# A transformer block on one core: the second part of k laid out over both partition halves without pinned matmuls, and every block of probabilities multiplied in two rounded parts

## The chip, the cores and the metric

The kernel runs on 1 core of one Trainium2 chip. The metric is the device time of one execution in microseconds (us). Three runs of the kernel before took 474.45, 476.0 and 477.67 us; the median is 476.0 us.

## The reference

Three blocks follow each other. First comes local attention with block summaries (2 batches, 8 heads, 768 positions, head size 64). Its output feeds the block that this change is about, a causal attention with four experts of 64 dimensions each, over two batches of 768 positions:

```python
for e in range(E):                       # E = 4 experts, K = 2 chosen per position
    q = x @ wq[e]; k = x @ wk[e]; v = x @ wv[e]
    scores = scale * (q @ k.transpose(0, 2, 1))
    scores = np.where(causal, -1e9, scores)
    scores = scores - scores.max(-1, keepdims=True)
    a = np.exp(scores); a /= a.sum(-1, keepdims=True) + 1e-09
    ye = a @ v @ wo[e]
    out += weight_of_expert_e_at_each_position * ye
```

A token and channel mixer follows: `u = x + relu(xt @ w_tok1) @ w_tok2` and `out = u + relu(u @ w_ch1) @ w_ch2`. The four mixer weights arrive as 64-bit floats, whose bits the kernel decodes on the chip.

## The kernel before, in words

**Precision.** Most operands are kept as two rounded parts, hi and lo, that TensorE takes at the rate of a single pass (the type fp32r in the trace). A product then is two or three such matmuls that add up in one PSUM bank. `split` (L91 to L93) makes the parts: ScalarE copies hi out of PSUM, VectorE writes lo as the difference. A matmul on plain float32 operands is one instruction in the program and two records in the trace.

**Stages.** `s1` is the local attention of one batch. `proj` makes q, k and v of the experts, `attn` the expert attention, `tokmix` the token mixer, `chmix` the channel mixer in passes of three weight blocks, and `load_ch` and `wt_load` load and decode weights. Decoding (`decode_w`, L115 to L135) is a ring of two raw buffers: a DMA from SyncE, then ScalarE, GpSimd, VectorE, ScalarE, GpSimd; the next load of a buffer waits for the last reader.

**What sets the order.** `run` interleaves generators when the program is written down: attention of batch 0 with the projection of batch 1 and the decoding of token weights, then attention of batch 1 with the token mixer, the decoding of the first channel weights and the first channel pass. A scheduler then orders every engine's instructions by its own model of their durations and picks buffers of the pools by when it thinks they come free. On the chip each engine goes through its list in that order. All DMAs are issued by SyncE, one after the other.

**Scores.** For experts e = 0 to 3 and the two halves h of the positions, `attn` computes scores of three row tiles. Two experts share the tiles of one pair p. `q2[p]` holds, for one expert, the hi part of q in the expert's own 64 partitions and the lo part in the other 64; `k2[p]` holds the hi part of k in both halves. So one matmul over 128 partitions (L368) gives (q hi + q lo) times k hi. The lo part of k is not copied: a second matmul (L366) reads the 64 partitions of `k2l` in which the projection left it, against q hi alone. Pins (`keep_in_program_order`) hold the matmuls of a group of two banks in a fixed order: first the 128-partition ones, then the 64-partition ones, then the pieces that share a bank. For h = 0 these are pieces of 128, 256 and 384 columns; for h = 1 pieces of 512, 128 and 256 columns in a first group and two of 512 in a second. VectorE masks each piece and takes its minimum (L374), ScalarE takes the exponential (L378), GpSimd normalises (L384).

**Values.** TensorE transposes each 128-wide block of probabilities (L394). Most blocks are split into `ph` and `pl` and multiplied with V in two matmuls (L404, L405). Blocks j = 0 and 3 of batch 0 and j = 3 of batch 1 instead are copied whole by ScalarE as `pf` (L398) and multiplied once as float32 (L399). That is 16 blocks, all 384 columns wide.

**Pools.** Big tiles have tag "b" (11 buffers of 6 KB per partition), half tiles tag "hf" (6 of 3 KB). The lo parts of k live in half tiles until their pair of experts is done.

Of the kernel before, what the change touches and what calls it, by code (L numbers as in the profile page):

```python
# [25 lines left out]
P = 128  # L26
# [3 lines left out]
NB = 3  # L30
NCH = NC1 // P // NB

NBIG, XB, MB, HB = 11, 8, 6, 6
BK = {"sc": 3, "pt": 3, "acc": 2}
NEGB = -8.0e9
BIG = 3.0e38
# [6 lines left out]
def stack_kernel(ctx: ExitStack, tc, qT, kT, kwT, vw, vT, wqkv, wo, tok1, tok2, ch1, ch2,  # L43
# [30 lines left out]
    def half(shape, dt, name):  # L74
        return big.tile(shape, dt, tag="hf", name=name, bufs=HB)
# [62 lines left out]
    def s1_load(b, hp, qb):  # L138
        first = b == 0 and hp == 0
        kx = unit([P, NT, KX], F32, f"kx{b}{hp}")  # L140
        kt = None
        if first:

            kt = xunit([P, S + 2 * WIN], F32, "kt")
            vec.memset(kx[:, 0, KW:KX], 0.0)
        vt = half([P, S], F32, "vt")
        vx = unit([P, NT, P], F32, f"vx{b}{hp}")
        loads = [(kt, kT) if first else (kx, kwT[b, hp])]
        loads += [(qb[i::2, :, i, :], qT[b, hp, i::2].rearrange("p (t c) -> p t c", c=P)) for i in range(2)]
# [124 lines left out]


    def proj(b, xh, xl, out):
        q2 = [unit([P, 2, S], F32R, f"q2{b}{i}") for i in range(2)]
        k2 = [unit([P, 2, S], F32R, f"k2{b}{i}") for i in range(2)]
        V = [unit([P, ST, 2, P], F32R, f"V{b}{i}") for i in range(2)]
        k2l = [None, None]  # L280
        out.extend((q2, k2, k2l, V))
        lg = gp.tile([P, ST, NE], F32, name="lg", bufs=1)
        for st in range(ST):
# [35 lines left out]


        for p in range(2):
            for c0, dst in ((0, q2), (1, k2)):
                hi, lo = (half([P, S], F32R, f"s{b}{p}{c0}{x}") for x in "hl")
                for h in range(2):
# [7 lines left out]
                    if h == 1:  # L332
                        for e in range(2):
                            own, other = slice(64 * e, 64 * e + 64), slice(64 - 64 * e, 128 - 64 * e)
                            nc.sync.dma_start(dst[p][own, e, :].bitcast(F32), hi[own].bitcast(F32))
                            nc.sync.dma_start(dst[p][other, e, :].bitcast(F32), (lo, hi)[c0][own].bitcast(F32))
                    yield
                if c0:
                    k2l[p] = lo

    def attn(b, q2, k2, k2l, V, wg, yT):
        for e in range(NE):
            pp, e0 = e // 2, 64 * (e % 2)
            es = slice(e0, e0 + 64)
            for h in range(2):
# [5 lines left out]
                    nk = P * (3 * h + r + 1)  # L351
                    prs.append((pre if h == 0 else sp).tile([P, nk], F32, name=f"pr{nk}", bufs=2))


                for gi, group in enumerate(((((0, 0, 128, 0), (1, 0, 256, 128)), ((2, 0, 384, 0),)),) if h == 0 else
                                           ((((0, 0, 512, 0),), ((1, 0, 128, 0), (2, 0, 256, 128))),
                                            (((1, 128, 640, 0),), ((2, 256, 768, 0),)))):
                    todo = [(a[:, o:o + c1 - c0], r, c0, c1, o > 0) for i, ts in enumerate(group)
                            for a in (bank("sc", f"s2s{b}{e}{h}{gi}{i}"),) for r, c0, c1, o in ts]

                    steps = [(t, 0) for t in todo if not t[4]] + [(t, 1) for t in todo if not t[4]]
                    steps += [(t, low) for t in todo if t[4] for low in (1, 0)]
                    for i, ((a, r, c0, c1, sec), low) in enumerate(steps):
                        qs = slice(P * (3 * h + r), P * (3 * h + r) + P)
                        if low:
                            mm = ten.matmul(a, q2[pp][es, e % 2, qs], k2l[pp][es, c0:c1], start=sec, stop=not sec)  # L366
                        else:
                            mm = ten.matmul(a, q2[pp][:, e % 2, qs], k2[pp][:, e % 2, c0:c1], start=not sec, stop=sec)  # L368
                        if i:
                            tc.keep_in_program_order(mm)  # L370
                    for a, r, c0, c1, _ in todo:
                        nk = P * (3 * h + r + 1)
                        ci, n = int(c0 > 0), c1 - c0
                        vec.tensor_tensor_reduce(prs[r][:, c0:c1], a, cmask[:, 512 - n:] if c1 == nk else cmask[:, :n],  # L374
                                                 scale=-0.125, scalar=mn[:, r, 0:1] if ci else BIG,
                                                 op0=ALU.add, op1=ALU.min, accum_out=mn[:, r, ci:ci + 1])
                        if c1 == nk:
# [11 lines left out]
                for j in range(nj):  # L389
# [3 lines left out]
                    for r in range(r0, 3):  # L393
                        ten.transpose(pT[:, P * r:P * r + P], prs[r][:, P * j:P * j + P], ident)  # L394
                    v = V[pp][:, j, e % 2, :]
                    if j in ((0, 3), (3,))[b]:
                        pf = sp.tile([P, HALF], F32, tag="ph", name="pf", bufs=3)
                        act.activation(pf[:, c0:], pT[:, c0:HALF], AF.Copy)  # L398
                        ten.matmul(acc[:, c0:HALF], v.bitcast(F32), pf[:, c0:], start=j == 0, stop=j == nj - 1)  # L399
                        continue  # L400
                    ph = sp.tile([P, HALF], F32R, tag="ph", name="ph", bufs=3)
                    pl = sp.tile([P, HALF], F32R, tag="pl", name="pl", bufs=3)
                    split(ph[:, c0:], pl[:, c0:], pT[:, c0:HALF])
# [264 lines left out]
```

## Time and profile before

| what | value |
|---|---|
| median of the runs shown | 476.0 us |
| the profiled execution's own time | 473.83 us |
| its span, first to last instruction | 471.9 us |
| PE busy / DVE / ACT / POOL | 446.6 / 283.5 / 231.0 / 283.3 us |
| mean granted TensorE clock | 0.980 of 2.4 GHz |
| chain that ended last, by engine | PE 79%, DMA 9%, DVE 5%, ACT 2%, issue 2%, POOL 1%, SP queue 1% |

PE is TensorE, DVE VectorE, ACT ScalarE, POOL GpSimd, SP SyncE. A matmul's record starts when it is issued and lasts through its pipeline, so two neighbouring records overlap, and a busy PE is not a PE at its peak. What a matmul costs in a stream is read from start to start. The chain of waits goes back from the last instruction to whatever released each step. In order of time the program has four stages: the inputs and local attention until about 94 us, attention of batch 0 until about 180 us, attention of batch 1 with the token mixer until about 250 us, and channel passes to the end.

### The profile page before, as it was taken

The numbers are of one execution on the slowest core, as the hardware profiler recorded it, in microseconds if no ns is written. First come the engines' busy times: TensorE is split into PE (matmuls) and PEld (weight loads), VectorE is DVE, ScalarE is ACT, GpSimd is POOL, SyncE is SP. The second block draws the span as 40 slices with busy tenths as digits, with TensorE's granted clock in tenths as the row PEclk, the third lists the DMA queues.
The fourth block names the chain that finished last, engine by engine and source line by source line (L and its number), as shares of the span: only waits on it lengthen the run. The fifth ranks groups of instructions, "written<-read, shape, count | busy, mean of one in ns | idle before, by whom it ended". The sixth has DMA issues, their size and how long they took to land.

```text
span 471.9 us, 8309 instructions
## 1 busy us (share of the span) xinstructions
PE 446.6 (95%) x2920; PEld 415.6 (88%) x2920; DVE 283.5 (60%) x821; ACT 231.0 (49%) x653; POOL 283.3 (60%) x319
## 2 busy tenths in 40 slices
PE   3778999999999998999999999999999999999996
PEld 3667999888787676889899999999999999999996
DVE  6777775658668749797796642645672673322322
ACT  1574975777777568868664333233323321110110
POOL 5664652658887875978895889787873772000000
PEclk9797999999999899999999999999999999999999
DMA  9999917504312932211211111212221110001111
GB/s 269 330 278 290 303 33 205 111 2 128 96 46 63 228 90 67 90 45 46 68 46 67 45 46 45 75 60 90 61 75 44 46 44 1 1 0 68 67 68 67
DMA packets 27704, 44.90 MB, mean 95 GB/s; under 512 B 2192, under 2 KB 19344, under 8 KB 27664
## 3 DMA queue, kind: packets, MB, share of 16 engines
q1 hardware_dynamic: 27664, 44.38, 32.4%
q8 instruction: 23, 0.38, 0.3%
q14 instruction: 17, 0.14, 0.1%
HBM read 34.93 MB, written 3.15 MB: 81 GB/s over the span
## 4 chain that ended last, share of the span: by engine, by line
PE 79%; DMA 9%; DVE 5%; ACT 2%; issue 2%; POOL 1%; SPq 1%; DVEq 0%; ACTq 0%
PE o L100 7%; PE h L101 7%; PE h L102 7%; PE o L101 7%; PE o L102 7%; PE h L100 7%; PE s1s L196 3%; DMA vt<-in_vT_dram 3%; PE s2p L394 3%; PE s2s L366 2%; DMA raw<-in_ch_dram 2%; PE s2s L368 2%; PE s1a L235 2%; PE pj L100 2%; PE s2a L399 2%; PE pj L102 2%
## 5 line engine op out<-in xcount | busy, mean ns | idle before, releaser
L96 ACT ACTIVATE hh<-h 128x384 fp32r<-128x384 f32 x48 | 23.5, 490 | 95.7 <-PE h L102 95.3
L126 POOL TENSOR_SCALAR deca<-deca 128x512 f32<-128x512 f32 x30 | 58.6, 1959 | 12.8 <-ACT deca L125 12.2
L101 PE MATMUL o<-hl,c2h 128*128 128x384 f32 x192 | 64.2, 336 | 0.0
L102 PE MATMUL o<-hh,c2l 128*128 128x384 f32 x192 | 64.2, 336 | 0.0
L497 DVE TENSOR_TENSOR oa<-o,oa 128x384 f32<-128x384 f32 x64 | 32.0, 549 | 52.7 <-PE o L102 52.7
L97 DVE SCALAR_TENSOR_TENSOR hl<-h,hh 128x384 fp32r<-128x384 f32 x48 | 26.4, 554 | 44.2 <-ACT hh L96 44.1
L100 PE MATMUL o<-hh,c2h 128*128 128x384 f32 x192 | 49.4, 336 | 0.0
L132 POOL TENSOR_TENSOR raw<-raw 128x512 f32<-128x512 f32 x30 | 32.3, 1076 | 25.8 <-DVE raw L129 23.5
L196 PE MATMUL s1s<-kx,qb 128*128 128x120 f32 x192 | 33.2, 337 | 13.0 <-DVE wvl L112 7.7
L208 ACT ACTIVATE pr<-n,mn 128x120 f32<-128x120 f32 x96 | 36.5, 383 | 15.2 <-DVE mn L205 15.2
L196 PEld LDWEIGHTS s1s<-kx,qb 128*128 128x128 f32 x192 | 31.1, 246 | 13.9 <-DVE wvl L112 7.7
L133 POOL TENSOR_TENSOR deca<-deca,raw 128x512 f32<-128x512 f32 x30 | 39.7, 1324 | 1.1
L384 POOL TENSOR_SCALAR pr<-pr,f,wg 128x128 f32<-128x128 f32 (+5 forms) x48 | 37.5, 791 | 2.0 <-DVE f L381 2.0
L101 PEld LDWEIGHTS o<-hl,c2h 128*128 128x128 f32 x192 | 36.0, 188 | 0.1
L102 PEld LDWEIGHTS o<-hh,c2l 128*128 128x128 f32 x192 | 36.0, 188 | 0.0
L131 ACT ACTIVATE raw<-raw 128x512 f32<-128x512 uint32 x30 | 20.2, 675 | 32.1 <-DMA raw<-in_ch_dram 30.8
L378 ACT ACTIVATE pr<-pr,mn 128x384 f32<-128x384 f32 (+5 forms) x48 | 31.8, 664 | 6.9 <-DVE mn L374 6.8
L100 PEld LDWEIGHTS o<-hh,c2h 128*128 128x128 f32 x192 | 34.8, 188 | 0.1
L100 PE MATMUL h<-u0h,c1h 128*128 128x384 f32 x96 | 32.5, 338 | 0.0
L101 PE MATMUL h<-u0l,c1h 128*128 128x384 f32 x96 | 32.4, 337 | 0.0
L100 PE MATMUL h<-u1h,c1h 128*128 128x384 f32 x96 | 32.3, 336 | 0.0
L102 PE MATMUL h<-u1h,c1l 128*128 128x384 f32 x96 | 32.3, 336 | 0.0
(206 smaller groups left out, 1296.5 us busy)
## 6 DMA issues: line engine op xcount, KB each, us to landing
raw<-in_ch_dram SPq DMA_DIRECT2D x24, 512.0 KB, 3.5
kx<-in_kwT_dram SPq DMA_DIRECT2D x7, 720.0 KB, 10.1
vx<-in_vw_dram SPq DMA_DIRECT2D x8, 576.0 KB, 10.5
qb<-in_qT_dram SPq DMA_DIRECT2D x16, 192.0 KB, 8.7
vt<-in_vT_dram SPq DMA_DIRECT2D x8, 384.0 KB, 10.1
raw<-in_tok_dram SPq DMA_DIRECT2D x6, 512.0 KB, 4.5
out_dram<-oa SPq DMA_DIRECT2D x16, 192.0 KB, 2.0
rqk<-in_wqkv_dram SPq DMA_DIRECT2D x4, 256.0 KB, 10.2
```

Source lines behind the costliest of these rows:

```text
L97: vec.scalar_tensor_tensor(lo, src, 0.0, hi.bitcast(F32), op0=ALU.max, op1=ALU.subtract)
L100: ten.matmul(out, lh, rh, start=start, stop=False)
L101: ten.matmul(out, lh, rl, start=False, stop=False)
L102: ten.matmul(out, ll, rh, start=False, stop=stop)
L126: gps.tensor_scalar(af, af, F64_TINY, F64_HUGE, op0=ALU.max, op1=ALU.min)
L132: gps.tensor_mul(lf, lf, ef)
L133: gps.tensor_add(af, af, lf)
L196: ten.matmul(sc[:, KX * i:KX * i + KX], qb[:, t // 2].rearrange("p i c -> p (i c)")[:, t % 2::2], kx[:, t, :], start=True, stop=True)
L208: act.activation(pr[:, i, :], n[:, i, :], AF.Exp, bias=mn[:, i:i + 1], scale=-1.0, accum_out=sm[:, i:i + 1])
L378: act.activation(prs[r], prs[r], AF.Exp, bias=mn[:, r, ci:ci + 1], scale=-1.0, accum_out=sm[:, r:r + 1])
L384: gps.tensor_scalar(prs[r][:, :nk], prs[r][:, :nk], f[:, r:r + 1], wg[:, 3 * h + r, e:e + 1], op0=ALU.mult, op1=ALU.mult)
L497: vec.tensor_add(oa[d], a[:, :HALF], oa[d])
```

## The change: what it does

The lo part of k gets tiles of the same form as `k2`: `k2l[p]` now is [128, 2, 768] with the lo part in both partition halves, filled by four more DMAs per pair and batch (16 in all, 192 KB each). The second score matmul reads 128 partitions like the first, so it also gives q lo times k lo. The pins go, and each score bank is written, and handed to VectorE, by itself. All blocks of probabilities are split; `pf` and the float32 matmul are gone. Big buffers become 12, half buffers 4; the v tile of the first two head pairs uses a buffer of the decoding ring; and the q and k tiles are allocated where each pair is projected. In the changed file lines after 145 have moved: score matmuls are L363, transposes L389, the value matmuls L394 and L395, DMAs of q and k L336, L337 and L340.

```diff
-NBIG, XB, MB, HB = 11, 8, 6, 6
+NBIG, XB, MB, HB = 12, 8, 6, 4
...
-        vt = half([P, S], F32, "vt")
+        vt = (dec.tile([P, S], F32, tag="raw", name="vt") if b == 0 and hp < 2 else half([P, S], F32, "vt"))
...
         for p in range(2):
+            for t, x in ((q2, "q2"), (k2, "k2"), (k2l, "k2l")):
+                t.append(unit([P, 2, S], F32R, f"{x}{b}{p}"))
...
                             nc.sync.dma_start(dst[p][other, e, :].bitcast(F32), (lo, hi)[c0][own].bitcast(F32))
+                            if c0:
+                                for half_ in (own, other):
+                                    nc.sync.dma_start(k2l[p][half_, e, :].bitcast(F32), lo[own].bitcast(F32))
                     yield
-                if c0:
-                    k2l[p] = lo
...
-                    steps = [(t, 0) for t in todo if not t[4]] + [(t, 1) for t in todo if not t[4]]
-                    steps += [(t, low) for t in todo if t[4] for low in (1, 0)]
-                    for i, ((a, r, c0, c1, sec), low) in enumerate(steps):
+                    a = bank("sc", f"s2s{b}{e}{h}{gi}")
+                    for r, c0, c1, o in ts:
                         qs = slice(P * (3 * h + r), P * (3 * h + r) + P)
-                        if low:
-                            mm = ten.matmul(a, q2[pp][es, e % 2, qs], k2l[pp][es, c0:c1], start=sec, stop=not sec)
-                        else:
-                            mm = ten.matmul(a, q2[pp][:, e % 2, qs], k2[pp][:, e % 2, c0:c1], start=not sec, stop=sec)
-                        if i:
-                            tc.keep_in_program_order(mm)
+                        for low, kk in enumerate((k2, k2l)):
+                            ten.matmul(a[:, o:o + c1 - c0], q2[pp][:, e % 2, qs], kk[pp][:, e % 2, c0:c1],
+                                       start=not low, stop=bool(low))
...
-                    if j in ((0, 3), (3,))[b]:
-                        pf = sp.tile([P, HALF], F32, tag="ph", name="pf", bufs=3)
-                        act.activation(pf[:, c0:], pT[:, c0:HALF], AF.Copy)
-                        ten.matmul(acc[:, c0:HALF], v.bitcast(F32), pf[:, c0:], start=j == 0, stop=j == nj - 1)
-                        continue
```

Three places show what the scheduler makes of it. In the names, s2s is a score bank, with batch, expert, half and group as its first digits; s2p is a bank of transposes and s2a a bank of the value product; the number behind the underscore counts buffers.

**TensorE, scores of batch 0, expert 0, second half, before:**

```order
L368 MATMUL s2s00100_1633<-k200_731,q200_729 128x512
L368 MATMUL s2s00101_1634<-k200_731,q200_729 128x128
L366 MATMUL s2s00100_1633<-s001l_1106,q200_729 128x512
L366 MATMUL s2s00101_1634<-s001l_1106,q200_729 128x128
L366 MATMUL s2s00101_1634<-s001l_1106,q200_729 128x256
L368 MATMUL s2s00101_1634<-k200_731,q200_729 128x256
```

and in the changed kernel:

```order
L363 MATMUL s2s0010_1638<-k200_1024,q200_1023 128x512
L363 MATMUL s2s0010_1638<-k2l00_1025,q200_1023 128x512
L363 MATMUL s2s0011_1643<-k200_1024,q200_1023 128x128
L363 MATMUL s2s0011_1643<-k2l00_1025,q200_1023 128x128
L363 MATMUL s2s0011_1643<-k200_1024,q200_1023 128x256
L363 MATMUL s2s0011_1643<-k2l00_1025,q200_1023 128x256
```

The count and the columns are the same. Each hi matmul is now followed at once by its lo matmul, with the same q block as weights and over the same partitions, and the first bank is complete after two matmuls, not after three.

**SyncE's queue between the two batches, before** (k201 is the k tile of batch 0's second pair, q210 and k210 are batch 1's first pair, raw64 a load of the decoding ring):

```order
L336 DMA k201_732<-s011h_1610 64x768
L122 DMA raw64_2087<-in_tok2_dram 128x2x512
L122 DMA raw64_2147<-in_tok2_dram 128x2x512
L122 DMA raw64_2210<-in_tok2_dram 128x2x512
L335 DMA q210_1520<-s100h_1911 64x768 x2
L336 DMA q210_1520<-s100l_1912 64x768 x2
L335 DMA k210_1522<-s101h_2068 64x768
L336 DMA k210_1522<-s101h_2068 64x768
```

and in the changed kernel:

```order
L340 DMA k2l01_1483<-s011l_1616 64x768 x2
L122 DMA raw64_2082<-in_tok1_dram 128x2x512
L122 DMA raw64_2114<-in_tok2_dram 128x2x512
L122 DMA raw64_2181<-in_tok2_dram 128x2x512
L122 DMA raw64_2247<-in_tok2_dram 128x2x512
L336 DMA q210_1929<-s100h_1932 64x768 x2
L337 DMA q210_1929<-s100l_1933 64x768 x2
L336 DMA k210_1930<-s101h_2095 64x768
L337 DMA k210_1930<-s101h_2095 64x768
L340 DMA k2l10_1931<-s101l_2096 64x768 x2
```

The last raw load for w_tok1, which stood ahead of the k201 copies, now stands behind them and behind four k2l copies. The scores of batch 1's first expert need two more copies behind the first two of k210.

**TensorE at the first scores of batch 1, before:**

```order
L368 MATMUL s2s10000_2499<-k210_1522,q210_1520 128x128
L368 MATMUL s2s10001_2500<-k210_1522,q210_1520 128x384
L366 MATMUL s2s10000_2499<-s101l_2069,q210_1520 128x128
L366 MATMUL s2s10001_2500<-s101l_2069,q210_1520 128x384
L366 MATMUL s2s10000_2499<-s101l_2069,q210_1520 128x256
L368 MATMUL s2s10000_2499<-k210_1522,q210_1520 128x256
L399 MATMUL s2a021_2223<-pf_2228,V01_734 128x384
```

and in the changed kernel:

```order
L363 MATMUL s2s1000_2555<-k210_1930,q210_1929 128x128
L363 MATMUL s2s1001_2564<-k210_1930,q210_1929 128x384
L417 MATMUL yt00_2613<-ident_76,yT0_1480 128x128
L394 MATMUL s2a021_2260<-ph_2265,V01_730 128x384
L389 MATMUL s2p0212_2281<-ident_76,pr512_2197 128x128
L389 MATMUL s2p0212_2281<-ident_76,pr640_2198 128x128
L389 MATMUL s2p0212_2281<-ident_76,pr768_2199 128x128
L363 MATMUL s2s1000_2555<-k2l10_1931,q210_1929 128x128
L363 MATMUL s2s1000_2555<-k210_1930,q210_1929 128x256
L363 MATMUL s2s1000_2555<-k2l10_1931,q210_1929 128x256
L363 MATMUL s2s1001_2564<-k2l10_1931,q210_1929 128x384
L395 MATMUL s2a021_2260<-pl_2266,V01_730 128x384
```

Five other matmuls now stand between the two that read k210 alone and the first that reads k2l10, and the whole float32 block (L399) has become two matmuls, the second of which reads VectorE's pl.

## Rows read from the trace of the kernel before

**Rows 1.** Busy us (instructions) by stretch, then granted clock, DMA share, GB/s.
```profile
core 0: us, PE busy (x) PEld busy (x) DVE busy (x) ACT busy (x) POOL busy (x), PEclk, DMA share, GB/s
94.00:150.00 56.00, 55.99 (x398) 47.76 (x397) 39.92 (x136) 41.08 (x118) 42.53 (x55) 1.00 0.24 67
150.00:192.00 42.00, 36.78 (x194) 27.97 (x194) 31.13 (x89) 30.22 (x76) 31.49 (x36) 0.96 0.49 126
...
192.00:252.00 60.00, 59.87 (x370) 53.79 (x370) 48.45 (x115) 43.59 (x105) 53.34 (x50) 1.00 0.17 54
252.00:396.00 144.00, 144.00 (x832) 143.40 (x832) 78.94 (x133) 49.74 (x92) 104.32 (x79) 1.00 0.17 56
```
**Rows 2.** Chain of waits, 150 to 245 us: start, length, what.
```profile
153.86 0.53 SPq L335
154.44 4.13 DMA k<-s101h
...
171.84 4.10 DMA raw<-in_ch_dram
...
215.02 3.62 DMA raw<-in_ch_dram
```
**Rows 3.** Timeline of TensorE, 113.5 to 122 us: start, length, instruction.
```profile
113.93 0.22 PE L405 MATMUL s2a<-pl,V 128*128 128x128 f32 x1
113.99 0.39 PE L102 MATMUL pj<-x0h,wqk1l 128*128 128x384 f32 x1
...
115.27 0.45 PE L368 MATMUL s2s<-k,q 128*128 128x128 f32 x2
...
116.47 0.28 PE L100 MATMUL pv<-wvh,x1h 128*128 128x260 f32 x1
116.59 0.28 PE L101 MATMUL pv<-wvl,x1h 128*128 128x260 f32 x1
...
118.38 0.31 PE L368 MATMUL s2s<-k,q 128*128 128x128 f32 x1
118.62 0.72 PE L366 MATMUL s2s<-s001l,q 64*128 64x512 f32 x3
...
119.49 0.49 PE L394 MATMUL s2p<-ident,pr 128*128 128x128 f32 x3
...
120.66 0.51 PE L368 MATMUL s2s<-k,q 128*128 128x512 f32 x1
...
121.75 0.59 PE L399 MATMUL s2a<-pf,V 128*128 128x384 f32 x1
```
**Rows 4.** Timeline of TensorE, 204 to 209 us, two matmuls of 512 columns.
```profile
205.58 0.40 PE L101 MATMUL g<-wol,zh 128*128 128x512 f32 x1
205.82 0.39 PE L102 MATMUL g<-woh,zl 128*128 128x512 f32 x1
```
**Rows 5.** Busy time by stretch of line 366 alone, the 64-partition matmuls.
```profile
94.00:150.00 56.00, 7.03 (x27) 3.94 (x27) 1.00 0.24 67
150.00:192.00 42.00, 5.82 (x21) 3.13 (x21) 0.96 0.49 126
192.00:252.00 60.00, 4.23 (x16) 2.36 (x16) 1.00 0.17 54
```
**Rows 6.** Chain of waits near 208 us: a block's matmul, rounded and whole.
```profile
208.16 0.18 PE s2a L405
...
208.80 0.65 PE s2a L399 x2
```
**Rows 7.** Busy time by stretch of line 399 alone, two records a block.
```profile
94.00:150.00 56.00, 5.06 (x12) 1.96 (x12) 1.00 0.24 67
150.00:192.00 42.00, 5.84 (x12) 2.11 (x12) 0.96 0.49 126
192.00:252.00 60.00, 3.34 (x8) 1.33 (x8) 1.00 0.17 54
```
**Rows 8.** Groups by line and shape: busy us, mean ns, then idle and releaser.
```profile
L93 DVE TENSOR_TENSOR pl<-s2p,ph 128x384 fp32r<-128x384 f32 x24 | 13.0, 550 | 1.9 <-ACT ph L92 1.8
```
**Rows 9.** Timeline of SyncE, 108 to 150 us, a load of the decoding ring.
```profile
113.56 0.39 SPq L122 DMA_DIRECT2D raw<-in_tok_dram  x1
```

More of the change, by code (lines that the diff above doesn't have):

```diff
@@ L276, in proj @@
     def proj(b, xh, xl, out):
-        q2 = [unit([P, 2, S], F32R, f"q2{b}{i}") for i in range(2)]
-        k2 = [unit([P, 2, S], F32R, f"k2{b}{i}") for i in range(2)]
         V = [unit([P, ST, 2, P], F32R, f"V{b}{i}") for i in range(2)]
-        k2l = [None, None]
+        q2, k2, k2l = [], [], []
         out.extend((q2, k2, k2l, V))
@@ L352, in attn @@
                     prs.append((pre if h == 0 else sp).tile([P, nk], F32, name=f"pr{nk}", bufs=2))
[L355 to L359, printed above, removed]
-                    steps = [(t, 0) for t in todo if not t[4]] + [(t, 1) for t in todo if not t[4]]
-                    steps += [(t, low) for t in todo if t[4] for low in (1, 0)]
-                    for i, ((a, r, c0, c1, sec), low) in enumerate(steps):
-                        qs = slice(P * (3 * h + r), P * (3 * h + r) + P)
-                        if low:
-                            mm = ten.matmul(a, q2[pp][es, e % 2, qs], k2l[pp][es, c0:c1], start=sec, stop=not sec)
-                        else:
-                            mm = ten.matmul(a, q2[pp][:, e % 2, qs], k2[pp][:, e % 2, c0:c1], start=not sec, stop=sec)
-                        if i:
-                            tc.keep_in_program_order(mm)
-                    for a, r, c0, c1, _ in todo:
@@ new lines, in attn @@
+                for gi, ts in enumerate((((0, 0, 128, 0), (1, 0, 256, 128)), ((2, 0, 384, 0),)) if h == 0 else
+                                        (((0, 0, 512, 0),), ((1, 0, 128, 0), (2, 0, 256, 128)),
+                                         ((1, 128, 640, 0),), ((2, 256, 768, 0),))):
+                    a = bank("sc", f"s2s{b}{e}{h}{gi}")
+                    for r, c0, c1, o in ts:
+                        qs = slice(P * (3 * h + r), P * (3 * h + r) + P)
+                        for low, kk in enumerate((k2, k2l)):
+                            ten.matmul(a[:, o:o + c1 - c0], q2[pp][:, e % 2, qs], kk[pp][:, e % 2, c0:c1],
+                                       start=not low, stop=bool(low))
+                    for r, c0, c1, o in ts:
@@ L372, in attn @@
                         nk = P * (3 * h + r + 1)
                         ci, n = int(c0 > 0), c1 - c0
-                        vec.tensor_tensor_reduce(prs[r][:, c0:c1], a, cmask[:, 512 - n:] if c1 == nk else cmask[:, :n],
+                        vec.tensor_tensor_reduce(prs[r][:, c0:c1], a[:, o:o + n],
+                                                 cmask[:, 512 - n:] if c1 == nk else cmask[:, :n],
                                                  scale=-0.125, scalar=mn[:, r, 0:1] if ci else BIG,
```

## The prediction

> **What bounds the kernel now.** I read the busy table by stretch first, because the mean over the span hides four different stages. [rows 1] holds the three stretches the change touches and, for comparison, one of channel passes. From 94 to 150 us PE is busy for 55.99 of 56 us and no other engine for more than 42.5: TensorE sets the pace. From 150 to 192 us PE is busy for only 36.78 of 42 us and its clock averages 0.96 of full, so something else holds it. From 192 to 252 us PE is at 59.87 of 60 again, but POOL stands at 53.34 and DVE at 48.45, so there is little room beside it. From 252 us on PE is full and nothing of that work changes.
>
> The chain of waits says what holds PE in the middle [rows 2]. At 153.86 us it stands in SyncE's queue, then for 4.13 us on the copy of k for batch 1's first expert; at 171.84 us on a raw weight load of 4.10 us that blocks ScalarE's list; at 215.02 us on another raw load of 3.62 us, in the decoding ring, although PE looks busy then. So before 150 us a microsecond of PE work is a microsecond of time; after that only a part of it is.
>
> **The change, part by part.** *Scores.* In the timeline of TensorE, start to start, the 64-partition matmuls are dear. The six matmuls of a first half (two each of 128, 256 and 384 columns) last from 115.27 to 116.47, 1.20 us [rows 3]. In the second half five matmuls (512 and 128 and 256 columns over 64 partitions, 128 and 256 over 128) last from 118.38 to 119.49, 1.11 us, and three of 512 columns, two of them over 64 partitions, from 120.66 to 121.75, 1.09 us [rows 3]. Matmuls over 128 partitions that follow each other cost 0.06 us at 128 columns, 0.12 at 260 [rows 3], 0.24 at 512 [rows 4] and 0.18 at 384 [rows 6]. After the change all are of that kind. The three sets become 2 x (0.06 + 0.12 + 0.18) = 0.72, 0.24 + 2 x 0.06 + 2 x 0.12 = 0.60 and 3 x 0.24 = 0.72 us. That saves 0.48 + 0.51 + 0.37 = 1.36 us per expert and batch, 10.9 us for eight.
>
> *Whole blocks.* A float32 block of 384 columns takes 0.65 us, a rounded matmul of the same width 0.18 [rows 6]. Two rounded ones take 0.36, so 0.29 us goes per block, 4.6 us for 16. PE loses 15.5 us in all.
>
> *Where these lie.* Of the 64-partition matmuls, eight per expert, 27 lie in 94 to 150 us, 21 in 150 to 192 and 16 in 192 to 252 [rows 5]; of the whole blocks 6, 6 and 4 [rows 7]. The saving by stretch is 27/8 x 1.36 + 6 x 0.29 = 6.3, then 3.6 + 1.7 = 5.3, then 2.7 + 1.2 = 3.9 us. The first counts in full. Of the second I take a third, 1.8, since the chain there leaves PE for long pieces. Of the third I take half, 2.0: PE is full, but POOL has only 6.7 us of idle time in 60 [rows 1], and the chain runs through the ring. Sum 10.1 us. The ends are 6.3 (nothing after 150 us) and 15.5 (all).
>
> *VectorE.* Each of the 16 blocks adds a subtraction of 0.55 us [rows 8]; ScalarE's copy stays, with another output. That is 3.3, 3.3 and 2.2 us by stretch. In the first two DVE has 16.1 and 10.9 us idle [rows 1], which hide it. In the last it has 11.6, beside a chain that is not PE's alone; I count half, 1.1 us. If the cover is gone, all 8.8 count. What comes late then is pl, and with it the second matmul of the block at the head of PE's list.
>
> *Copies of k's lo part.* 16 more DMAs. Issues of these copies follow each other every 0.58 us on SyncE (153.86 to 154.44 [rows 2]), so each pair of experts holds the queue 2.3 us longer. For batch 0 the copies stand behind all loads of the local attention, and PE has projections to do; I cost them at nothing. At batch 1's first expert PE already waits for the copies, and the two lo copies are issued third and fourth: 1.2 us more. The five matmuls that the new order puts in front hide part of it at best. Bounds: 0, and 2.3 us if the whole pair is waited for.
>
> *The raw load that moved.* It was issued at 113.56 us [rows 9], and now goes out after eight copies of k and its lo part. GpSimd's list has its first step later too, so I cost it at nothing by itself; the cover is that the token weights are needed only by the token mixer, late in the next stretch. If that goes, it is the second rival.
>
> *Order and buffers.* Without pins the first score bank is ready for VectorE one matmul sooner, and the scheduler has dealt all buffers anew. No row prices a new order. The nearest is the stall of 150 to 192 us: 42 - 36.78 = 5.2 us idle and 0.04 x 42 = 1.7 us of lost clock. It may go, or come a second time; I take zero and keep +/-6.9 us.
>
> Net: 10.1 - 1.1 - 1.2 = 7.8 us. The profiled execution took 473.83 us, so it would take 466.0. It lies 2.2 us below the median of the runs shown; against the median 476.0 the forecast is **468 us**.
>
> **The rivals.**
> 1. *TensorE stays the pace throughout.* All 15.5 us count, 460.5 us, and less if the stall goes too. For: PE is full in two of three stretches. Against: the chain after 150 us.
> 2. *The other engines keep their pace.* SyncE's queue holds four raw loads ahead of the copies of q and k for batch 1, and each load waits until the ring has a free buffer, that is for POOL and DVE. The first of them goes out at least four issues, 2.3 us, later, and the decoding has as much work as before. What PE gains before 150 us it then waits for at batch 1's first scores: 10.1 - 6.3 - 1.2 = 2.6 us remain, 473 us. For: POOL is busy for 42.5 of 56 and 53.3 of 60 us. Against: POOL has 13.5 us idle before 150 us.
> 3. *Slower: VectorE becomes the bound.* With 12 more subtractions before 192 us it is busy for 39.92 + 3.3 of 49.7 us and 31.13 + 3.3 of about 40, 86 to 87%. Its list is in order, and pl, masks, lo parts of the projections and three decoding steps share it. If each of the 12 lands in the path, 6.6 us are added, the saving before 192 us does not appear, and the lo copies cost 1.2: 476.0 + 6.6 + 1.2 - 2.0 = 482 us. This decides once DVE's share in 94 to 150 us passes some 90%.
> 4. *The score matmuls get no cheaper.* In the channel passes 832 matmuls over 128 partitions take 144 us, 173 ns each, with 143.4 us of weight loads beside them [rows 1]: loads for the same 128 rows overlap a matmul in flight. If they did not for the new lo matmuls, only the whole blocks would count: 1.7 + 0.6 + 0.6 - 2.3 = 0.6 us, 475.4 us. The Trainium skill, "TensorE: Matmul & The Clock Gate", part on packing small matmuls, states that weight loads overlap with running matmuls only when their row groups differ; by that rule the second matmul of a pair would wait like the 64-partition one does now. The rows speak against it.
>
> That the change does not do what it says is ruled out by the order: no pf is left, and every score matmul reads k or k2l.
>
> **How the numbers follow.** A measurement of this kernel tells about 1% from no change, 4.8 us. Forecast (462 to 471 us) 0.53; rival 1 0.14; rival 2 0.20; rival 3 0.09; rival 4 0.04. The range: from the forecast down by the 5.4 us that were not counted (15.5 - 10.1) and by some of the stall to 458; up by the stall's second coming and into rival 2 to 477. Some 0.15 is left outside, rival 3 and the bottom of rival 1. The forecast's own range is 462 to 471. Faster by over 1% means below 471.2: nearly all of the forecast and rival 1, 0.65. Within 1%: rivals 2 and 4 and a rest, 0.25. Slower: rival 3 and a disordered schedule, 0.10.
>
> **What would show it.** Score matmuls over 128 partitions 0.24 us apart at 512 columns, hi to lo: else rival 4. The 16 blocks as pairs of 0.18 us. PE busy in full up to batch 1's first scores, and those some 6 us earlier than 158.6 us, where the copy of k landed (154.44 + 4.13 [rows 2]); if they are not earlier, rival 2 holds. DVE's share before 150 us under 90%, else rival 3. The chain at batch 1's start on the copy of k's lo part, about 1 us longer than now on k. The stretch of channel passes unchanged at 173 ns a matmul. Wrong would be a stall of another kind: ScalarE or SyncE stuck on a load that the new order put earlier.

## The result: 1.1% slower, with less work on TensorE

The changed kernel takes 481.4 us in the median of four runs (478.57 to 482.8) against 475.2 us (473.92 to 477.67): ratio 1.0108, interval 1.0062 to 1.0155. The forecast was 468 us, and the range ended at 477. The profiled execution took 478.57 us, with a span of 476.8 us and a mean granted clock of 0.974. Ratios here and below leave out single executions that took over 1.5% more than the fastest of their kernel; medians are of all.

The busy times of the changed kernel by the stretches of [rows 1]: us, busy (instructions) of PE, weight loads, DVE, ACT and POOL, granted clock, DMA share, GB/s.

```profile
94.00:150.00 56.00, 53.47 (x402) 49.43 (x400) 43.54 (x143) 42.10 (x123) 43.99 (x55) 0.97 0.29 81
150.00:192.00 42.00, 34.43 (x192) 27.91 (x191) 34.75 (x95) 28.55 (x73) 36.35 (x37) 0.92 0.62 163
192.00:252.00 60.00, 55.98 (x342) 51.05 (x341) 46.85 (x115) 42.81 (x104) 49.98 (x46) 0.97 0.17 54
252.00:396.00 144.00, 143.88 (x835) 142.96 (x834) 82.15 (x130) 49.08 (x94) 104.73 (x80) 1.00 0.17 56
```

The channel passes are what they were. In the three stretches before them PE now idles, and its clock falls: 55.99 became 53.47, 59.87 became 55.98. To compare kernels I cut at events instead of fixed times: stretch A runs from the first score matmul of batch 0 to the first of batch 1, stretch B from there to the last value matmul. The same columns, the kernel before:

```profile
93.70:158.80 65.10, 63.37 (x434) 52.99 (x433) 46.72 (x155) 46.87 (x131) 50.66 (x63) 1.00 0.30 81
158.80:247.00 88.20, 84.57 (x493) 71.80 (x494) 68.73 (x179) 65.23 (x163) 72.06 (x72) 0.98 0.26 74
```

and the changed kernel:

```profile
94.10:158.10 64.00, 59.28 (x436) 54.22 (x434) 50.83 (x162) 48.25 (x136) 51.74 (x62) 0.97 0.35 93
158.10:251.60 93.50, 84.10 (x493) 73.67 (x494) 74.32 (x190) 64.71 (x161) 78.09 (x76) 0.95 0.33 92
```

Take from each length the idle time of PE and the clock's loss, (1 - clock) x length. What is left is PE's busy time at full clock. In A it fell from 63.4 to 57.4 us, about the 6.3 us that the prediction expected before 150 us. But the idle time rose from 1.7 to 4.7 and the clock's loss from 0 to 1.9, so A became only 1.1 us shorter. In B the busy time fell by 3.4 us, idle time rose by 5.8 and the clock's loss by 2.9: B became 5.3 us longer. 5.3 - 1.1 = 4.2 us is nearly all of the 4.7 us between the two profiled executions, and all of it arises in B.

Who PE and its weight loads wait for in the changed kernel, 94 to 252 us: total us, times, longest.

```profile
PE s2a L395 <- DVE pl L93: 5.7, 7, 1.8
PE s2a L394 <- ACT ph L92: 2.5, 2, 2.2
...
PEld s2a L395 <- DVE pl L93: 10.1, 15, 2.1
PEld s2a L394 <- ACT ph L92: 4.0, 5, 2.5
PEld s2s L363 <- DVE mn L368: 3.0, 5, 1.2
```

Before, none of PE's listed waits in these 158 us was on pl. One of the new ones can be followed. TensorE's timeline, start, length, instruction, and the wait in brackets:

```profile
135.27 0.33 PE L394 MATMUL s2a<-ph,V 128*128 128x384 f32 x1
137.42 0.45 PE L395 MATMUL s2a<-pl,V 128*128 128x384 f32 x1 [1.81 <-DVE pl L93]
...
138.33 0.53 PE L100 MATMUL pj<-x1h,wqk1h 128*128 128x384 f32 x1
138.65 0.53 PE L101 MATMUL pj<-x1l,wqk1h 128*128 128x384 f32 x1
...
142.74 0.34 PE L102 MATMUL pj<-x1h,wqk0l 128*128 128x384 f32 x1
142.91 0.34 PE L100 MATMUL pj<-x1h,wqk0h 128*128 128x384 f32 x1
```

VectorE in the same time:

```profile
134.84 1.26 DVE L127 TENSOR_SCALAR deca<-deca 128x512 int32<-128x512 int32 x1 [0.63 <-POOL deca L126]
136.02 0.28 DVE L93 TENSOR_TENSOR V<-pv,V 128x128 fp32r<-128x128 f32 x1
136.22 0.67 DVE L128 SCALAR_TENSOR_TENSOR deca<-raw,deca 128x512 int32<-128x512 int32 x1
136.82 0.54 DVE L93 TENSOR_TENSOR pl<-s2p,ph 128x384 fp32r<-128x384 f32 x1
```

and ScalarE's copy that made ph:

```profile
134.57 0.48 ACT L92 ACTIVATE ph<-s2p 128x384 fp32r<-128x384 f32 x1
```

ph was ready at 135.05 us. The subtraction stood in VectorE's list behind two steps of the decoding and a part of V; the first step had itself waited for GpSimd. So pl started 1.8 us late, PE stood still, and then ran its 384-column matmuls 0.32 us apart where it needs 0.17. The granted clock of PE, in pieces of 2 us:

```profile
136.00:138.00 2.00, 0.58 (x5) 1.00 0.01 4
138.00:140.00 2.00, 2.00 (x9) 0.51 0.33 66
140.00:142.00 2.00, 2.00 (x9) 0.64 0.54 197
142.00:144.00 2.00, 2.00 (x14) 1.00 0.03 8
```

After the wait PE ran for about 3.4 us at the lower of its two levels (1.2 GHz), then at 2.4 again. VectorE's load around it, the kernel before (columns as above):

```profile
130.00:142.00 12.00, 11.99 (x72) 10.18 (x71) 8.19 (x29) 8.88 (x25) 9.87 (x12) 1.00 0.14 45
142.00:154.00 12.00, 11.43 (x65) 9.52 (x64) 10.42 (x36) 8.67 (x24) 9.45 (x10) 1.00 0.28 78
```

and the changed kernel:

```profile
130.00:142.00 12.00, 9.61 (x52) 8.63 (x51) 11.31 (x31) 8.39 (x23) 11.35 (x12) 0.86 0.15 45
142.00:154.00 12.00, 10.49 (x65) 9.08 (x64) 11.86 (x36) 9.16 (x24) 10.15 (x11) 1.00 0.30 86
```

VectorE went from 18.6 to 23.2 of these 24 us, though over 94 to 150 us its share is only 78%. Subtractions are only a small part of that: 66 instructions stand there instead of 64, the ones that write pl take 4.6 us instead of 3.4, but the three decoding steps (L127 to L129) 6.6 instead of 3.1, because there are eight of them instead of six and some last longer beside GpSimd.

This pause lies in A. It is one of four of more than 1.5 us that PE makes in A and B, where the kernel before makes one, of 2.28 us up to 178.3 us. The other three lie in B. Two of them:

```profile
177.46 0.44 PE L394 MATMUL s2a<-ph,V 128*128 128x384 f32 x1 [2.18 <-ACT ph L92]
...
209.55 0.56 PE L395 MATMUL s2a<-pl,V 128*128 128x384 f32 x1 [1.71 <-DVE pl L93]
```

The first is the longest of all and has nothing to do with a subtraction. ph came late because ScalarE, whose list is in order too, had stood for a load of channel weights:

```profile
175.43 0.66 ACT L125 ACTIVATE deca<-raw 128x512 f32<-128x512 f32 x1 [1.41 <-DMA raw<-in_ch_dram]
```

Ahead of the second pause, pl stood in VectorE's list behind a decoding step of 1.27 us, as in A:

```profile
207.75 1.27 DVE L129 TENSOR_SCALAR raw<-deca 128x512 int32<-128x512 int32 x1
```

After both the granted clock fell, which cost about 3.4 and 1.7 us:

```profile
178.00:180.00 2.00, 1.84 (x8) 0.75 1.04 270
180.00:182.00 2.00, 1.35 (x3) 0.50 1.02 247
182.00:184.00 2.00, 1.86 (x9) 0.50 0.51 152
184.00:186.00 2.00, 2.00 (x10) 0.54 0.00 2
...
210.00:212.00 2.00, 2.00 (x9) 0.50 0.00 0
212.00:214.00 2.00, 2.00 (x9) 0.72 0.12 25
```

The last of the four, 1.57 us up to 240.22 us, waited for VectorE's u0l; the clock stayed at 1.00.

### The profile page after: what moved, and what is told of

It is laid out like the page before. It is cut to its first block, busy times and chain, and to the rows that moved or that the text cites. A ratio compares the mean times of both kernels' runs of the same rounds, so it can differ in the third digit from the quotient of the medians.

```text
span 476.8 us, 8366 instructions
## 1 busy us (share of the span) xinstructions
PE 440.2 (92%) x2920; PEld 416.8 (87%) x2920; DVE 295.3 (62%) x837; ACT 229.8 (48%) x653; POOL 288.0 (60%) x319
## 5 line engine op out<-in xcount | busy, mean ns | idle before, releaser
L96 ACT ACTIVATE hh<-h 128x384 fp32r<-128x384 f32 x48 | 23.2, 488 | 80.1 <-PE h L102 80.1
L197 PE MATMUL s1s<-kx,qb 128*128 128x120 f32 x192 | 31.4, 324 | 14.4 <-DMA qb<-in_qT_dram 8.0
L132 POOL TENSOR_TENSOR raw<-raw 128x512 f32<-128x512 f32 x30 | 31.6, 1052 | 19.5 <-DVE raw L129 17.3
L197 PEld LDWEIGHTS s1s<-kx,qb 128*128 128x128 f32 x192 | 29.2, 232 | 15.3 <-DVE wvl L112 8.0
L379 POOL TENSOR_SCALAR pr<-pr,f,wg 128x128 f32<-128x128 f32 (+5 forms) x48 | 42.1, 889 | 0.1
L133 POOL TENSOR_TENSOR deca<-deca,raw 128x512 f32<-128x512 f32 x30 | 40.7, 1356 | 1.1
L373 ACT ACTIVATE pr<-pr,mn 128x128 f32<-128x128 f32 (+5 forms) x48 | 32.0, 669 | 10.3 <-DVE mn L368 10.2
L93 DVE TENSOR_TENSOR pl<-s2p,ph 128x384 fp32r<-128x384 f32 (+2 forms) x72 | 32.4, 460 | 5.1 <-ACT ph L92 4.9
L127 DVE TENSOR_SCALAR deca<-deca 128x512 int32<-128x512 int32 x30 | 26.8, 893 | 13.9 <-POOL deca L126 13.8
L389 PE MATMUL s2p<-ident,pr 128*128 128x128 f32 x168 | 31.3, 284 | 2.1 <-DVE u0l L93 1.6
L92 ACT ACTIVATE ph<-s2p 128x384 fp32r<-128x384 f32 (+2 forms) x72 | 29.3, 417 | 7.5 <-PE s2p L389 5.4
## 6 DMA issues: line engine op xcount, KB each, us to landing
vx<-in_vw_dram SPq DMA_DIRECT2D x8, 576.0 KB, 10.9
rqk<-in_wqkv_dram SPq DMA_DIRECT2D x4, 256.0 KB, 10.6
```

The lines of the kernel that those rows point to most:

```text
L93: vec.tensor_sub(lo, src, hi.bitcast(F32))
L132: gps.tensor_mul(lf, lf, ef)
L133: gps.tensor_add(af, af, lf)
L197: ten.matmul(sc[:, KX * i:KX * i + KX], qb[:, t // 2].rearrange("p i c -> p (i c)")[:, t % 2::2], kx[:, t, :], start=True, stop=True)
L373: act.activation(prs[r], prs[r], AF.Exp, bias=mn[:, r, ci:ci + 1], scale=-1.0, accum_out=sm[:, r:r + 1])
L379: gps.tensor_scalar(prs[r][:, :nk], prs[r][:, :nk], f[:, r:r + 1], wg[:, 3 * h + r, e:e + 1], op0=ALU.mult, op1=ALU.mult)
```

## The experiments

Each ratio is to the kernel before, timed beside it. First came four that undo or isolate one part. Theory V was that VectorE's subtractions cost what the cheaper matmuls gave; rival K, that the copies, the lost pins or the new buffers did it.

**Only the scores (whole blocks put back in the changed kernel).**

```diff
+                    if j in ((0, 3), (3,))[b]:
+                        pf = sp.tile([P, HALF], F32, tag="ph", name="pf", bufs=3)
...
+                        continue
```

> The second part of k in both halves, no pins, the new buffers; but the 16 blocks stay whole float32 as before. Theory V (the 16 added subtractions on VectorE are what TensorE waits for, and the waits cost clock): faster than before, 465 to 472 us, the waits of L395 on pl fall from 10 us to under 2. Rival K (the copies of k's lo part, the lost pins and the new buffers cost the time): no faster than the changed kernel less a little, 477 to 483 us.

475.1 us, ratio 1.0009 [0.9969, 1.0050], between the two expectations. The K = 128 scores (matmuls over 128 partitions), with their copies and new buffers and without pins, bring nothing that can be measured.

**Only the splitting (the kernel before without its whole blocks).** The five lines above taken out of the kernel before.

> The kernel before, with all 16 whole blocks split in two parts and nothing else. Theory V: slower than before, 478 to 486 us, waits on pl appear at L405. Rival K: 4.6 us less matmul work and nothing against it, 471 to 476 us.

479.8 us, 1.0086 [1.0040, 1.0132]: slower, as theory V has it.

**Pins and groups of two banks put back in the changed kernel.**

```diff
+                    steps = [(t, 0) for t in todo if not t[4]] + [(t, 1) for t in todo if not t[4]]
...
+                        if i:
+                            tc.keep_in_program_order(mm)
```

> The changed kernel with the grouped banks and pins of before put back on its 128-partition matmuls. Theory V: as the changed kernel, 478 to 484 us, since VectorE's load is the same. Rival K, if the lost pins are its part: back to 471 to 476 us.

472.2 us, 0.9907 [0.9868, 0.9947]: faster than both kernels, and against theory V, by which nothing should have changed.

**No subtraction for the 16 blocks.** The second matmul of these blocks reads ph again, so their hi part counts twice in the output and their lo part is left out.

```diff
+                    if j in ((0, 3), (3,))[b]:
+                        act.activation(ph[:, c0:], pT[:, c0:HALF], AF.Copy)
+                        ten.matmul(acc[:, c0:HALF], v, ph[:, c0:], start=j == 0, stop=False)
+                        ten.matmul(acc[:, c0:HALF], v, ph[:, c0:], start=False, stop=j == nj - 1)
+                        continue
```

> The changed kernel, but the 16 blocks take no subtraction: their second matmul reads the hi part once more, so TensorE and ScalarE do the same work and VectorE 8.8 us less; the product of these blocks is then not the reference's. Theory V: 463 to 472 us. Rival K: 477 to 482 us.

473.6 us, 0.9960 [0.9923, 0.9998], again between the two. These four seemed to add up: subtractions +8 us, missing pins +9. The next four tested that.

**Pins and whole blocks together (K = 128).** The pinned kernel with pf put back.

> The kernel with 128-partition score matmuls in the pinned groups (472.2 us), and in addition the 16 blocks whole again. Theory A, that pins and unsplit blocks each count by themselves: 16 subtractions of 0.55 us go from VectorE, 8.8, and PE takes 4.6 back; splitting cost +4.6 and +6.3 us in the two pairs that ran, so 466 to 468 us. Rival B, that the pins already cured what the subtractions did: the whole blocks cost PE 4.6 us more and nothing comes back, 475 to 477 us. A wait of PE on pl of more than 1 us should be gone under A.

476.6 us, 0.9973 [0.9929, 1.0016]. The 466 to 468 us of the theory that is called A there fell: the parts do not add.

**The kernel before without its pins.**

```diff
-                        if i:
-                            tc.keep_in_program_order(mm)
```

> The kernel before with its pins taken out and nothing else. If the pins themselves are worth what their return brought in the changed kernel (9.2 us): about 484 us. If it was the writing of two banks as one group, or a schedule that falls out well or badly by chance: within 3 us of 475.

477.3 us, 1.0031 [0.9997, 1.0066]: pins are not worth 9 us. PE's busy time at full clock in A and B rose from 146.2 to 153.9 us, yet the stretches grew by only 1.9, because idle time fell from 5.4 to 1.4 and the clock's loss from 1.8 to 0.

**Groups of two banks without pins (K = 128, split).** The same two lines out of the pinned kernel.

> The 128-partition scores written in groups of two banks, first matmuls before second ones, as in the run of 472.2 us, but without pins; all blocks split. If the written order in groups carries the gain: about 472 us. If the pins carry it: about 481 us, as the changed kernel.

475.7 us, 0.9987 [0.9939, 1.0035]: between the two.

**Subtractions made, but not read by the 16 blocks.** Their hi part counts twice in the output here, too.

```diff
-                    ten.matmul(acc[:, c0:HALF], v, pl[:, c0:], start=False, stop=j == nj - 1)
+                    x = ph if j in ((0, 3), (3,))[b] else pl
+                    ten.matmul(acc[:, c0:HALF], v, x[:, c0:], start=False, stop=j == nj - 1)
```

> The changed kernel with all subtractions in place, but the second matmul of the 16 blocks reads ph, so that PE never waits for these 16 pl (the product then lacks their lo part). If the 7.8 us between the changed kernel and the one without the 16 subtractions are PE's wait for pl: about 473.5 us. If they are VectorE's time, which also delays masks, decoding and the release of the transposed bank: about 480 us, near the changed kernel's 481.4. Between: both.

481.2 us, 1.0082 [1.0032, 1.0131], near the changed kernel: without the wait, but with VectorE's work, next to nothing comes back. The weight loads' wait for pl went from 10.1 to 2.6 us, and the one for ph rose from 4.0 to 9.1:

```profile
PEld s2a L394 <- ACT ph L92: 9.1, 11, 2.5
...
PEld s2a L396 <- DVE pl L93: 2.6, 7, 1.0
```

Take one wait away and another takes its place.

**Relief for VectorE elsewhere, and relief for GpSimd.** In the first, the 16 adds of the value product are gone, and with them the product with the lo part of V; in the second, 8 normalisations, so that these probabilities go on unnormalised.

```diff
...
-                act.activation(tmp[es], acc[o0:o0 + 64, :HALF], AF.Copy)
-                vec.tensor_add(yT[es, pp, HALF * h:HALF * h + HALF], acc[es, :HALF], tmp[es])
+                act.activation(yT[es, pp, HALF * h:HALF * h + HALF], acc[es, :HALF], AF.Copy)
```

```diff
-                for r in range(3):
+                for r in range(3 - h):
```

> The changed kernel without the final add on VectorE (16 instructions of 0.55 us, 8.8 us in all; the result then lacks the product with the lo part of V; ScalarE's copy stays, with another output). PE, ScalarE and GpSimd do what they did. If VectorE's total time is what the 16 subtractions overran: back to 473 to 475 us, as without the subtractions. If only the subtractions' own place ahead of TensorE matters: 480 to 482 us.

> The changed kernel with GpSimd relieved instead: for the second half of the positions the third row tile is not normalised, 8 instructions of about 1 us less, 8 us in all (these probabilities then go on unnormalised). If GpSimd's pace, with the decoding on it, sets the time: 473 to 475 us. If VectorE does: 480 us or more.

474.8 us (0.9962 [0.9915, 1.0008]) and 474.9 us (0.9975 [0.9934, 1.0015]). Taking 8 us from GpSimd brought the time down as far as taking 8.8 from VectorE, so nothing here singles out VectorE. And each is one order: the next runs ask what an order is worth.

**The same instructions in another order.** The first two score banks of the second half trade places, in the changed kernel and in the pinned one.

```diff
-                                         (((0, 0, 512, 0),), ((1, 0, 128, 0), (2, 0, 256, 128)),
+                                         (((1, 0, 128, 0), (2, 0, 256, 128)), ((0, 0, 512, 0),),
```

> The changed kernel with the first two score banks of the second half written in the other order: the bank of 128 and 256 columns ahead of the bank of 512. The instructions are the same, only the scheduler's order changes. If the schedule by chance is worth little: 480 to 483 us. If an order alone moves as much as the pins did (9 us): anything from 472 to 485 us.

> The kernel of 472.2 us (128-partition scores in pinned groups, all blocks split) with the same swap of the first two banks. If the gain of the pins is a matter of what they hold together: 471 to 474 us. If that kernel was a lucky order: 475 us or more.

475.8 us (0.9995 [0.9959, 1.0030]) and 480.1 us (1.0114 [1.0076, 1.0153]). The swap makes the changed kernel faster and the pinned one slower, each by more than the intervals. Stretches A and B of the pinned kernel (its profiled execution took 479.01 us and reached A at 102.2 us, 8 us later than the changed kernel's, so only its stretches are compared):

```profile
102.20:163.70 61.50, 57.88 (x435) 52.98 (x433) 47.94 (x157) 44.45 (x128) 47.45 (x60) 1.00 0.35 92
163.70:251.20 87.50, 80.50 (x493) 72.07 (x494) 73.72 (x191) 66.33 (x164) 71.61 (x71) 0.98 0.34 91
```

and with the swap:

```profile
92.90:156.90 64.00, 59.78 (x435) 54.77 (x434) 49.58 (x155) 43.97 (x128) 46.41 (x60) 0.97 0.34 88
156.90:251.70 94.80, 84.25 (x496) 75.21 (x494) 74.56 (x192) 67.41 (x167) 73.99 (x72) 0.95 0.33 89
```

VectorE has the same work to within 2.5 us of 122, and PE's busy time at full clock is 136.7 and 137.4 us. The difference of 9.8 us is idle time (10.6 to 14.8) and clock (1.8 to 6.7).

**Such orders for each arithmetic.** In the kernel before: the same swap; the two banks of the first half swapped; the turn of PSUM banks for projections begun one step later. In the changed kernel: first-half banks swapped; last two banks swapped. In the K = 128 kernel with whole blocks: the first swap.

```diff
-    rr, rc = (rot(("sc", "pt", "acc", "sc", "pt")) for _ in range(2))
+    rr, rc = rot(("pt", "acc", "sc", "pt", "sc")), rot(("sc", "pt", "acc", "sc", "pt"))
```

```diff
-                                          ((1, 128, 640, 0),), ((2, 256, 768, 0),))):
+                                          ((2, 256, 768, 0),), ((1, 128, 640, 0),))):
```

> The kernel before with its first two score banks of the second half swapped; instructions the same. If the kernel before stands at the good end of its orders: 477 to 482 us. If its pinned score groups make it insensitive: 474 to 477.

> The kernel before with the two score banks of the first half swapped. If the kernel before is at the good end of its orders: 477 to 482 us. If it is insensitive: 474 to 477.

> The kernel before with the turn of PSUM banks that projections and mixer use begun one step later. If the kernel before is at the good end of its orders: 477 to 482 us. If it is insensitive: 474 to 477.

> The changed kernel with the two score banks of the first half swapped. If the changed kernel's 481.4 us is an unlucky order: 472 to 478 us. If its arithmetic is slow: 480 to 484.

> The changed kernel with the last two score banks of the second half swapped. If its 481.4 us is an unlucky order: 472 to 478 us. If its arithmetic is slow: 480 to 484.

> The 128-partition kernel with whole blocks and no pins (475.1 us), with the first two score banks of the second half swapped. If whole blocks leave VectorE room, so that its order matters little: 473 to 477 us. If the order matters as much as with split blocks: outside of that.

475.7 us (0.9997 [0.9963, 1.0031]), 472.7 (0.9946 [0.9901, 0.9990]) and 483.8 (1.0172 [1.0097, 1.0247]) for the kernel before; 483.7 (1.0149 [1.0088, 1.0209]) and 484.0 (1.0192 [1.0143, 1.0240]) for the changed one; 474.9 (0.9994 [0.9950, 1.0038]) for the last. Of the kernel before, the first came in as forecast for an insensitive kernel, the second below both ranges and the third above both; the two of the changed kernel as if its arithmetic were slow, which the first swap (475.8 us) speaks against; the last as forecast. The third was not harmless: PE's work at full clock rose to 152.3 us, so it stays out of the means below, and so does the kernel before without pins with its 153.9 us. That is a choice: with these two the mean ratio of the 64-partition kernels would be 1.0029 instead of 0.9981. All in one table, worked out as above from one profiled execution each, some of which reached A late (the changed kernel's first swap at 99.8 us, its last banks swapped at 100.9); the clock column is good to about 0.5 us per stretch.

| arithmetic, order | ratio | A + B, us | PE at full clock | PE idle | clock's loss |
|---|---|---|---|---|---|
| 64 partitions, whole: before | 1 | 153.4 | 146.2 | 5.4 | 1.8 |
| first swap | 0.9997 | 153.7 | 145.9 | 5.7 | 2.0 |
| first half swapped | 0.9946 | 150.9 | 146.3 | 4.6 | 0 |
| not in the means: no pins | 1.0031 | 155.3 | 153.9 | 1.4 | 0 |
| not in the means: turn of banks | 1.0172 | 164.8 | 152.3 | 8.7 | 3.8 |
| 64 partitions, split: pins | 1.0086 | 156.0 | 143.2 | 9.1 | 3.7 |
| 128, whole: no pins | 1.0009 | 151.1 | 141.1 | 10.1 | 0 |
| pins | 0.9973 | 151.9 | 140.1 | 11.8 | 0 |
| no pins, first swap | 0.9994 | 149.6 | 140.6 | 8.9 | 0 |
| 128, split: changed kernel | 1.0108 | 157.4 | 136.7 | 14.1 | 6.6 |
| first swap | 0.9995 | 155.0 | 136.0 | 13.5 | 5.5 |
| first half swapped | 1.0149 | 159.1 | 138.9 | 14.5 | 5.7 |
| last banks swapped | 1.0192 | 160.2 | 138.6 | 16.8 | 4.8 |
| groups, no pins | 0.9987 | 155.0 | 137.4 | 12.1 | 5.6 |
| groups and pins | 0.9907 | 149.0 | 136.7 | 10.6 | 1.8 |
| groups and pins, first swap | 1.0114 | 158.8 | 137.4 | 14.8 | 6.7 |

A + B of the K = 128 kernel with whole blocks and the first swap, to read beside those of the changed kernel:

```profile
96.90:160.30 63.40, 60.08 (x435) 53.14 (x433) 47.78 (x155) 47.85 (x133) 52.60 (x63) 1.00 0.37 97
160.30:246.50 86.20, 80.57 (x493) 70.75 (x494) 69.56 (x181) 64.91 (x161) 75.54 (x74) 1.00 0.36 98
```

Means over orders: PE's work falls from 146.1 to 140.6 to 137.4 us, and A + B goes from 152.7 to 150.9 to 156.4. What PE no longer does it waits; with split blocks it waits, in the mean, more than it saved, and its clock falls as well. The step from whole to split is +5.5 us of A + B, with a 95% interval of about 1.8 to 9.2 from the scatter of the seven and the three orders. In timed ratios the means are 0.9981, 0.9992 and 1.0065. The last step, 0.7% or 3.5 us, is no larger than the scatter allows by chance (interval about -0.2 to 1.7%), so by the timed runs alone it is not settled. And only three of the seven split orders were also run with whole blocks. Pair by pair (no pins, pins, first swap) splitting changed the time by +0.99, -0.66 and +0.01%, and at 64 partitions by +0.86%; A + B changed by +6.3, -2.9, +5.4 and +2.6 us. The mean of the four pairs, 0.3% and 2.9 us, is not clear of zero in either. What the splitting costs is open; a gain of 1.8 us, as forecast, does not show.

## Why the prediction was wrong, step by step

- **"So before 150 us a microsecond of PE work is a microsecond of time" failed.** It rested on PE's 55.99 of 56 us in [rows 1]. The work did go, 6.0 us in A, but 4.9 came back as idle time, in which PE waited for the engines that feed it, and as lower clock. It is so over all orders: in the mean of the three 64-partition and the seven split kernels of the table PE's work in A falls from 63.5 to 57.7 us, and A itself only from 65.4 to 63.8. The kernel before without pins shows it from the other side: 7.7 us more PE work, 1.9 us more time. A full engine in the trace was no proof that the others could go faster.
- **The score term was too large.** The 512-column matmuls are 0.23 us apart, hi to lo, in the place that is shown first here, as forecast, but in only five of 24 places. In the median they are 0.31 us apart: mostly short transposes stand right ahead, as in the second place:

```profile
129.46 0.40 PE L363 MATMUL s2s<-k,q 128*128 128x512 f32 x1
129.69 0.39 PE L363 MATMUL s2s<-k2l,q 128*128 128x512 f32 x1
129.92 0.22 PE L363 MATMUL s2s<-k,q 128*128 128x128 f32 x1
...
117.42 0.48 PE L363 MATMUL s2s<-k,q 128*128 128x512 f32 x1
117.74 0.39 PE L363 MATMUL s2s<-k2l,q 128*128 128x512 f32 x1
```

  And in the median the pieces of 128, 256 and 384 columns cost 0.11, 0.17 and 0.24 us, where 0.06, 0.12 and 0.18 were taken from [rows 3] and [rows 6]. From start to start, waits included, all score records add up to 34.3 us before and 26.7 after: 7.6 of the 10.9 us. PE's work at full clock fell by 5.5 (146.1 to 140.6). None of it shows in the timed mean (0.9981 to 0.9992; with the two kernels that stay out, 1.8 us would), where with the copies 6 us were counted.
- **"In the first two DVE has 16.1 and 10.9 us idle, which hide it" failed.** The idle time was there, but not where the subtractions came due: 97% busy from 130 to 154 us, and mostly with other work. The blocks and their subtractions, counted at -2.9 + 1.1 us together, stand at +5.5 us in the profiles and +3.5 in the timed means, but at +2.9 and +1.4 in the four pairs of like order. PE's own part was smaller than counted as well: splitting took 3.2 us from its work (140.6 to 137.4), not 4.6.
- **"Order and buffers", taken as zero, was mis-sized, though not by much.** The changed kernel's own order stands 0.43%, 2.0 us, above the mean of its seven. The bound of 6.9 us was about right: they span 0.9907 to 1.0192, 4.4 us below to 9.1 above the kernel before. The stall of 150 to 192 us, from which the bound was taken, grew: 7.6 us idle and 3.4 us of lost clock instead of 5.2 and 1.7.
- **The copies** cost less than the 1.2 us taken, within their bounds. Batch 1's first scores begin at 158.09 us, and PE waits twice, 1.4 us together against 1.2 before:

```profile
158.09 0.53 PE L363 MATMUL s2s<-k,q 128*128 128x128 f32 x2 [0.80 <-DMA k<-s101h]
...
159.84 0.30 PE L363 MATMUL s2s<-k2l,q 128*128 128x128 f32 x1 [0.61 <-DMA k2l<-s101l]
```

  They were to begin some 6 us earlier than 158.6 us; that they did not is what the prediction named as the sign of its second rival.
- **The rivals.** The second, other engines keep their pace, describes the scores: time unchanged while PE waits. SyncE's queue, its proposed carrier, is not what PE waits for most. The third, VectorE as the bound, gave 482 us, but its condition, 90% from 94 to 150 us, was not met (78%), and relief for GpSimd came out the same. The fourth fell: the score matmuls did get cheaper, by 7.6 us. The Trainium skill, "TensorE: Matmul & The Clock Gate", part on packing small matmuls, has weight loads overlap with running matmuls only when their row groups differ; this trace does not agree, since the two matmuls at 129.46 and 129.69 us, over the same rows, are 0.23 us apart although each has a weight load of 0.19 us of its own. The stall of another kind, which the prediction named as the sign of being wrong, was there too: ScalarE on a raw load before 177.46 us. A load of channel weights held ScalarE there in the kernel before as well ([rows 2], 171.84 us), but the clock did not fall after it.

Summed up by the timed means, which add up to the ratio of 1.0108 by the way they are made: scores +0.5 us, where -6.0 were counted; splitting +3.5, where -1.8 were; this kernel's own order +2.0, and the kernel before stands 0.9 us above the mean of its three: 5.1 us slower, where 7.8 us faster were forecast.

What stays open: that VectorE, ScalarE and GpSimd are tied to TensorE in a chain without slack is argued from the waits, not shown. Each relief is one order, and three of the seven split orders (0.9907 to 0.9995) are about as fast without any. What makes an order good was not found. The raw load that moved was not tried by itself. Nor were four of the seven split orders run with whole blocks.

The pinned, split kernel is the fastest that was run, 472.2 us. Its swap costs 8 us, so what it has is above all a good order; the kernel before with its first-half banks swapped comes to 472.7 us with nothing else changed.

## What to carry to other kernels

Before counting saved matmul time as saved time, look at who feeds TensorE in pieces of some 10 us, because idle time of a feeding engine averaged over a stage hides nothing where its list is full. Ask also what fills it: here it was decoding more than the new subtractions. Where a scheduler deals the order anew, run a few harmless swaps of both versions: here they moved the same instructions by almost 3%, more than the change was worth. And compare like order with like order: of four such pairs one was faster with split blocks, two slower and one the same. Whether a small float32 matmul that spares another engine an instruction is the better bargain, though TensorE does it more slowly, is not settled here.

## What the runs showed of the hardware

- After the 1.81 us wait the clock fell to half for some 3.4 us, so the pause cost about 3.5 us instead of 1.8. After those of 2.18 and 1.71 us it fell as well. Not every pause does it: the 2.28 us up to 178.3 us in the kernel before and the 1.57 us up to 240.22 us in the changed one were followed by a granted clock of 1.00.
- Over the runs that enter the ratios the mean granted clock was 0.980 to 0.984 in the three K = 128 kernels with whole blocks and 0.970 to 0.981 in the seven with split ones.
- VectorE's first decoding step (L127) took 0.42 us at 110.97 us, with GpSimd idle, and as little, 0.43 us, at 129.50 us beside GpSimd's normalisation (L379). It took 1.26 us while GpSimd ran this:

```profile
134.78 1.03 POOL L132 TENSOR_TENSOR raw<-raw 128x512 f32<-128x512 f32 x1
```

  The Trainium skill, "SBUF — State Buffer", section on the two separate sides, says that VectorE, in a mode that uses two ports, and GpSimd take one shared port pair as an exclusive lock: whichever starts first has it for its whole instruction, and the other blocks. The trace agrees beside L132, since the step ended 0.29 us after GpSimd's; beside L379 it does not, since the step started 0.04 us after GpSimd's and was not held up.
